# Chunked attention before a SwiGLU-like feed-forward: four 64x64 TensorE tiles, token order by GpSimd, wider v loads, two load queues, and a new order of the first loads

## The chip, the cores and the metric

The kernel runs on one core of a Trainium2 chip. The metric is the device time of one execution in microseconds. The kernel before takes 379.26 us (median of 3 runs, 377.64 to 379.83). A run over 1.5% above the fastest of its kernel counts as slow and is left out. The span that a profile shows is about 2 us shorter than the timed run (377.2 against 378.91 us in the profiled run of before).

## The reference, cut to what matters

```python
batch, n_heads, seq, head_dim = (8, 8, 576, 64)          # attention in chunks of 64 tokens, 9 per sequence
scores = scale * np.matmul(q_c, k_c.transpose(0, 1, 2, 4, 3))     # 64x64 for each chunk and head
attn = np.exp(scores - max) / sum
out = np.matmul(attn, v_c)
# then, over all 8*576 = 4608 tokens, with x = out of all heads side by side (4608 x 512):
h = x @ w_in                                             # 512 -> 2048
g = h * (1.0 / (1.0 + np.exp(-beta * h)))
return (g @ w_out).astype(np.float32)                    # 2048 -> 512
```

All inputs and the output are float32; the kernel multiplies in bfloat16. q, k and v are 9.4 MB each, w_in and w_out 4.2 MB each.

## The kernel before

The tokens are cut into 9 blocks of 512 (8 chunks of 64, all 8 heads). For each block the kernel loads q, k and v, casts them, transposes q and k so that the head dimension lies on the partitions, computes scores, exponentials, V products and their normalization into `xT`, and then two large products: `mm1` (w_in, 16 groups of 4 matmuls) and `mm2` (w_out, the same size). Instructions are emitted in the order of an invented time, `at(time, f, ...)`; every engine runs its own in that order and waits on semaphores for what it needs. One unit of that time is one group of mm1 and, from block 1 on, one group of mm2. So the schedule is a static order for each engine, and an instruction that waits holds up all that follow it on the same engine.

```python
def load_qk(blk, h0, n_h):                  # q on partitions 0-63, k on 64-127; 8 tokens (2 KB) in a piece
    ...
        r = 64 * which + 8 * at
        return e.dma_start(qkstage[r:r + 8 * n, s, h0:h0 + n_h, :],
                           a.rearrange("h (p i) d -> p h (i d)", i=8))
    P.dma("sp", f, ...)
...
def order_k(blk, hp, eng):                  # k alone is put into token order; q is read with a stride
    P.op(eng, lambda e: e.tensor_copy(
        kT[:, hp, :, :, :].rearrange("k c p i -> k (c p) i"),
        qkT[:, :, hp, 64:128].rearrange("k i t -> k t i")), ...)
...
def scores(blk, hp):
    for c in range(8):
        for hb in range(2):                 # two diagonal tiles: rows r and columns r
            r = slice(64 * hb, 64 * hb + 64)
            e.matmul(A[r, hp, 64 * c:64 * c + 64],
                     kT[r, hp, c, :, :].rearrange("k p i -> k (p i)"),
                     qkT[r, :, hp, 8 * c:8 * c + 8].rearrange("k i p -> k p i"))
...
# first loads: q, k, v of block 0; w_in; q, k, v of block 1; then w_out
at(-96, load_qk, 1, 0, 8)
at(-95, load_v, 1)
```

The softmax here doesn't subtract the row's maximum and nothing guards it: scores larger than these inputs give would overflow.

Of the kernel before, what the change touches and what calls it, by code (L numbers as in the profile page):

```python
# [157 lines left out]
def bass_chunk_attention__then__act_swish_beta_kernel(nc, q, k, v, w_in, w_out, beta, out):  # L158
# [8 lines left out]
    with ExitStack() as es:  # L167
# [7 lines left out]
        selsum = sb("selsum", [128, 8], F32)  # L175
        sel = sb("sel", [128, 8, 64], BF16)
# [9 lines left out]
        vstage = sb("vstage", [128, NVS, 4, 8, 64], F32)  # L186
        qkcast = sb("qkcast", [128, 8, H, 64], BF16)
        qkT = sb("qkT", [128, 8, 4, 128], BF16)
        kT = sb("kT", [128, 4, 8, 8, 8], BF16)
        NVA = 2  # L190
        v_bf = sb("v_bf", [128, NVA, 4, 8, 64], BF16)
# [27 lines left out]

        def make_constants():  # L220
# [6 lines left out]
            for b in range(4):  # L227
# [5 lines left out]
            ident = identity[:, :].rearrange("p (m g x y) -> p m g x y", m=4, g=2, x=2)  # L233
            P.op("dve", lambda e: e.tensor_reduce(
                selsum[:, :], ident[:, :, 0, :, :].rearrange("p m x y -> p y m x"),
                mybir.AxisListType.XY, ALU.add), reads=[K("identity")], writes=[K("selsum")])
            P.op("dve", lambda e: e.tensor_single_scalar(
                sel[:, :, :], selsum[:, :].unsqueeze(2).to_broadcast([128, 8, 64]), -1.0, ALU.mult),
                reads=[K("selsum")], writes=[K("sel")])
            P.op("dve", lambda e: e.tensor_reduce(  # L240
                mask[:, :], ident[:, :, :, 1, :].rearrange("p m g y -> p m g y"),
                mybir.AxisListType.XYZ, ALU.add), reads=[K("identity")], writes=[K("mask")])
# [12 lines left out]
        def load_qk(blk, h0, n_h):  # L255
            s = blk % NQS
            for which, src in ((0, q), (1, k)):
                for b, c, n, at in chunk_runs(blk):
                    def f(e, which=which, src=src, b=b, c=c, n=n, at=at):
                        a = src[b][h0:h0 + n_h, 64 * c:64 * (c + n), :]  # L260
                        r = 64 * which + 8 * at
                        return e.dma_start(qkstage[r:r + 8 * n, s, h0:h0 + n_h, :],  # L262
                                           a.rearrange("h (p i) d -> p h (i d)", i=8))
                    P.dma("sp", f, writes=[K("qkstage", s, hp, which, at, v=blk)
                                           for hp in range(h0 // 2, (h0 + n_h) // 2)])

        def load_v(blk):
            s = blk % NVS
            for b, c, n, at in chunk_runs(blk):
                for h in range(H):  # L270
                    def f(e, b=b, c=c, n=n, at=at, h=h):
                        a = v[b, h][64 * c:64 * (c + n), :]
                        r = 64 * (h % 2)
                        return e.dma_start(vstage[r:r + 64, s, h // 2, at:at + n, :],  # L274
                                           a.rearrange("(c j) d -> j c d", j=64))
                    P.dma("sp", f, writes=[K("vstage", s, at, h, v=blk)])
# [29 lines left out]
        def cast_w_out(j, engines):  # L306
            s = (4 + j) % NWS
            for i, eng in enumerate(engines):
                dst = w_out_bf[:, 4 * j + i, :]
                src = wstage[:, s, 512 * i:512 * (i + 1)]  # L310
                if eng == "act":
                    P.op("act", lambda e, d=dst, a=src: e.activation(d, a, AF.Copy, scale=0.5),
                         reads=[K("wstage", s, v=4 + j)], writes=[K("w_out", 4 * j + i)])
                else:
                    P.op(eng, lambda e, d=dst, a=src: e.tensor_single_scalar(d, a, 0.5, ALU.mult),  # L315
                         reads=[K("wstage", s, v=4 + j)], writes=[K("w_out", 4 * j + i)])
# [22 lines left out]
        def order_k(blk, hp, eng):  # L339
            P.op(eng, lambda e: e.tensor_copy(  # L340
                kT[:, hp, :, :, :].rearrange("k c p i -> k (c p) i"),
                qkT[:, :, hp, 64:128].rearrange("k i t -> k t i")),
                reads=[K("qkT", hp, v=blk)], writes=[K("kT", hp, v=blk)])

        def transpose_pe(blk, hp, eng):
            dst = A[:, hp, :].bitcast(BF16).rearrange("p (i t) -> p i t", i=8)
            for i in range(8):
# [3 lines left out]
                    reads=[K("qkcast", hp, v=blk), K("identity")], writes=[K("A", hp, v=("t", blk))])  # L351
            for which, out, src in (
                    ("kT", kT[:, hp, :, :, :].rearrange("k c p i -> k (c p) i"),
                     dst[:, :, 64:128].rearrange("k i t -> k t i")),
                    ("qkT", qkT[:, :, hp, 0:64], dst[:, :, 0:64])):
                if eng == "act":
                    P.op("act", lambda e, out=out, src=src: e.activation(out, src, AF.Copy),
                         reads=[K("A", hp, v=("t", blk))], writes=[K(which, hp, v=blk)])
                else:
                    P.op("dve", lambda e, out=out, src=src: e.tensor_copy(out, src),  # L360
                         reads=[K("A", hp, v=("t", blk))], writes=[K(which, hp, v=blk)])

        def cast_v(blk, eng, hp):
            s, sa = blk % NVS, blk % NVA
            keys = [K("vstage", s, at, h, v=blk) for _, _, _, at in chunk_runs(blk)
                    for h in (2 * hp, 2 * hp + 1)]
            P.op(eng, lambda e: e.tensor_copy(v_bf[:, sa, hp, :, :], vstage[:, s, hp, :, :]),  # L367
                 reads=keys, writes=[K("v_bf", sa, hp, v=blk)])

        def scores(blk, hp):  # L370
            for c in range(8):
                for hb in range(2):
                    def f(e, c=c, hb=hb):
                        r = slice(64 * hb, 64 * hb + 64)
                        return e.matmul(A[r, hp, 64 * c:64 * c + 64],  # L375
                                        kT[r, hp, c, :, :].rearrange("k p i -> k (p i)"),
                                        qkT[r, :, hp, 8 * c:8 * c + 8].rearrange("k i p -> k p i"))
                    P.op("pe", f, reads=[K("qkT", hp, v=blk), K("kT", hp, v=blk)],
                         writes=[K("A", hp, v=("s", blk))])

        def exp(blk, hp):
            P.op("act", lambda e: e.activation(E[:, hp, :], A[:, hp, :], AF.Exp, scale=0.125),  # L382
                 reads=[K("A", hp, v=("s", blk))], writes=[K("E", hp, v=blk)])
# [19 lines left out]
        def spread(blk, hps, banks):  # L403
            for b in range(4):
                for hp, bank in zip(hps, banks):
                    P.op("pe", lambda e, b=b, hp=hp, bank=bank: e.matmul(  # L406
                        A[:, bank, 128 * b:128 * b + 128],
                        sel[32 * hp:32 * hp + 32, 2 * b:2 * b + 2, :].rearrange("p h d -> p (h d)"),
                        Rs[32 * hp:32 * hp + 32, :], tile_position=(32 * hp, 0)),
                        reads=[K("Rs", v=blk), K("sel")], writes=[K("A", bank, v=("r", blk, hp))])  # L410

        def attend(blk, hp, bank):
            sa = blk % NVA
            for c in range(8):
                for hb in range(2):
                    def f(e, c=c, hb=hb):
                        r = slice(64 * hb, 64 * hb + 64)
                        return e.matmul(A[r, bank, 64 * c:64 * c + 64],  # L418
                                        v_bf[r, sa, hp, c, :], E[r, hp, 64 * c:64 * c + 64])
                    P.op("pe", f, reads=[K("E", hp, v=blk), K("v_bf", sa, hp, v=blk)],  # L420
                         writes=[K("A", bank, v=("o", blk, hp))])

        def copy_o(blk, hp, bank):
            P.op("act", lambda e: e.activation(o_sb[:, hp % 2, :], A[:, bank, :], AF.Copy),  # L424
                 reads=[K("A", bank, v=("o", blk, hp))], writes=[K("o_sb", hp % 2, v=(blk, hp))])

        def normalize(blk, hp, bank):
            sx = blk % NXT
            P.op("dve", lambda e: e.tensor_tensor(  # L429
                xT[:, sx, hp, :], o_sb[:, hp % 2, :], A[:, bank, :], ALU.mult),  # L430
                reads=[K("o_sb", hp % 2, v=(blk, hp)), K("A", bank, v=("r", blk, hp))],
                writes=[K("xT", sx, hp, v=blk)])


        def mm1(blk, t, bank):
            sx, sg, T = blk % NXT, blk % 2, NT * blk + t
            for c in range(NC):
# [3 lines left out]
                    reads=[K("w_in", t // 4, c), K("xT", sx, c, v=blk)],  # L441
# [8 lines left out]
        def mm2(blk, s, part, bank):  # L450
# [6 lines left out]
            if part == 3:  # L457
                P.op("act", lambda e: e.activation(ostage[:, N % NOS, :], F[:, bank, :], AF.Copy),  # L458
# [11 lines left out]
        def attention(blk, t0, u):  # L470
# [3 lines left out]
            for hp in range(4):  # L474
# [112 lines left out]
```

## Time and profile before

In the tables and profile lines, PE is TensorE (PEld its weight loads), DVE is VectorE, ACT is ScalarE and POOL is GpSimd; L453 is a line of the kernel, and `[19.19 <-POOL w_out_bf L315]` says that the engine stood idle for 19.19 us before and what ended the wait. A "large matmul" is one of mm1 or mm2; "spread" is the matmuls that copy the reciprocals of the softmax sums over the partitions; beta is the input that scales h in the sigmoid.

| Stretch of the span (us) | What runs | PE busy |
|---|---|---|
| 0-26 | loads, block 0's attention | little |
| 26-61 | block 0's mm1, block 1's attention | 26.3 of 35.1 us |
| 61-82 | wait for w_out, behind q, k, v of blocks 1 and 2 | 1.6 of 20.8 us |
| 82-97 | first mm2 groups, paced by w_out casts | 10.3 of 14.9 us |
| from 97 | mm1 of one block interleaved with mm2 of the one before | 33.5 of 34.0 us for a block |

From the page's busy slices of before (each digit is the busy share of a fortieth of the span in tenths; PEclk is the granted clock of TensorE in tenths; the last row is GB/s):

```profile
PE   1669584026898999999999999999999999999996
...
PEclk9999955558999989999999999999999999999999
DMA  8999999977879988849995994897250100001012
```

The load is busy in all of the first slices while PE has a hole in slices 7 to 9. The stretches (columns: stretch, its length, busy time and count of PE, PE's weight loads, DVE, ACT and POOL, granted clock, DMA share, GB/s) show two loading rates and the full stage:

```profile
15.00:20.00 5.00, 5.00 (x103) 4.80 (x100) 1.88 (x4) 2.43 (x5) 1.23 (x2) 1.00 1.28 234
20.00:25.00 5.00, 2.52 (x63) 1.74 (x59) 3.19 (x5) 1.59 (x3) 0.61 (x1) 1.00 1.05 386
...
199.00:233.00 34.00, 33.47 (x287) 17.38 (x290) 14.84 (x23) 17.20 (x28) 11.41 (x14) 1.00 0.81 159
```

The timeline of PE shows what ended the hole, and the chain of waits one block's scores:

```profile
82.10 2.06 PE L453 MATMUL F<-w_out_bf,g 128*128 128x512 bf16 x4 [19.19 <-POOL w_out_bf L315]
```

```profile
199.04 3.63 PE A L375 x64
```

In the trace these 64 matmuls start in pairs 110 ns apart, while pairs of V products, whose operands are dense, start some 30 ns apart.

### The profile page before, as it was taken

How to read it: one execution, taken by the hardware profiler on the slowest of the kernel's cores; microseconds unless marked ns; L12 is line 12 of the kernel's file. 1: busy time of each engine (PE TensorE's matmuls, PEld its weight loads, DVE VectorE, ACT ScalarE, POOL GpSimd, SP SyncE). 2: the span in 40 equal slices, each digit the busy share in tenths (PEclk: the TensorE clock that was granted, in tenths of full speed). 3: DMA queues.
4: the chain of work that ended last, by engine and by line, in shares of the span. 5: the costliest groups of instructions: out<-in, count | busy, mean ns of one | idle time of the engine just before them, and what ended most of it. 6: DMA issues, size and time to landing. Idle time of an engine off the chain costs nothing.

```text
span 377.2 us, 6314 instructions
## 1 busy us (share of the span) xinstructions
PE 320.5 (85%) x2621; PEld 166.1 (44%) x2656; DVE 148.3 (39%) x245; ACT 167.9 (45%) x271; POOL 95.2 (25%) x111
## 2 busy tenths in 40 slices
PE   1669584026898999999999999999999999999996
PEld 0544272001364544464446445544644464444442
DVE  2357625002325426433642454255236425544310
ACT  2438462002454345536553654545365536444521
POOL 0211230069643364063042405226040000000000
PEclk9999955558999989999999999999999999999999
DMA  8999999977879988849995994897250100001012
GB/s 151 201 385 195 153 298 261 143 113 156 160 179 198 207 184 189 178 118 202 138 176 123 188 181 113 176 202 155 61 108 30 56 22 36 30 28 57 28 56 85
DMA packets 89053, 53.91 MB, mean 143 GB/s; under 512 B 71104, under 2 KB 71104, under 8 KB 89024
## 3 DMA queue, kind: packets, MB, share of 16 engines
q1 hardware_dynamic: 81776, 44.05, 59.0%
q10 hardware_dynamic: 7248, 9.45, 8.0%
q8 instruction: 21, 0.34, 0.4%
q14 instruction: 8, 0.07, 0.1%
HBM read 36.71 MB, written 9.44 MB: 122 GB/s over the span
## 4 chain that ended last, share of the span: by engine, by line
PE 72%; SPq 14%; DMA 6%; DVE 3%; issue 2%; POOL 2%; ACT 1%; POOLq 0%
PE F L453 32%; PE F L438 29%; SPq L274 8%; PE A L375 7%; DMA qkstage<-in_k_dram 5%; SPq L262 5%; PE A L418 2%; PE A L406 1%; POOL w_out_bf L315 1%; POOL qkcast L329 1%; ACT tt L443 1%; DVE g L446 1%; DMA vstage<-in_v_dram 1%; SPq L283 1%; PE A L388 1%
## 5 line engine op out<-in xcount | busy, mean ns | idle before, releaser
L446 DVE SCALAR_TENSOR_TENSOR g<-tt,F 128x512 bf16<-128x512 bf16 x144 | 98.7, 687 | 183.8 <-ACT tt L443 183.8
L453 PE MATMUL F<-w_out_bf,g 128*128 128x512 bf16 x553 | 145.0, 384 | 26.6 <-POOL w_out_bf L315 20.9
L443 ACT ACTIVATE tt<-F,beta_half 128x512 bf16<-128x512 f32 x144 | 98.7, 687 | 148.9 <-PE F L438 148.4
L438 PE MATMUL F<-xT,w_in_bf 128*128 128x512 bf16 x564 | 148.6, 389 | 3.1 <-DVE g L446 0.9
L453 PEld LDWEIGHTS F<-w_out_bf,g 128*128 128x128 bf16 x576 | 55.1, 98 | 93.9 <-POOL w_out_bf L315 23.7
L438 PEld LDWEIGHTS F<-xT,w_in_bf 128*128 128x128 bf16 x576 | 55.7, 100 | 70.6 <-issue 5.0
L329 POOL CAST qkcast<-qkstage 128x1024 bf16<-128x1024 f32 x31 | 31.5, 1056 | 105.7 <-DMA qkstage<-in_k_dram 105.7
L340 POOL COPY kT<-qkT 128x512 bf16<-128x512 bf16 x28 | 28.8, 1069 | 49.8 <-DMA qkT<-qkcast 49.8
L375 PE MATMUL A<-qkT,kT 64*64 64x64 bf16 x576 | 33.3, 283 | 0.0
L375 PEld LDWEIGHTS A<-qkT,kT 64*64 64x64 bf16 x576 | 31.0, 127 | 3.4 <-issue 2.1
L458 ACT ACTIVATE ostage<-F 128x512 f32<-128x512 f32 x36 | 21.5, 597 | 22.0 <-PE F L453 22.0
L424 ACT ACTIVATE o_sb<-A 128x512 f32<-128x512 f32 x36 | 21.3, 594 | 13.0 <-PE A L418 7.9
L429 DVE TENSOR_TENSOR xT<-o_sb,A 128x512 bf16<-128x512 f32 x36 | 24.1, 681 | 2.6 <-PE A L406 2.6
L382 ACT ACTIVATE E<-A 128x512 bf16<-128x512 f32 x36 | 21.2, 595 | 7.0 <-PE A L375 3.9
L367 POOL CAST v_bf<-vstage 128x512 bf16<-128x512 f32 x34 | 20.5, 621 | 14.5 <-PE A L375 5.8
L348 PE MATMUL A<-identity,qkcast 128*128 128x128 bf16 x64 | 7.3, 292 | 17.4 <-DVE qkcast L329 8.5
L348 PEld LDWEIGHTS A<-identity,qkcast 128*128 128x128 bf16 x64 | 5.7, 132 | 18.9 <-DVE qkcast L329 8.8
L406 PE MATMUL A<-Rs,sel 32*128 32x128 bf16 x144 | 8.5, 235 | 6.4 <-DVE Rs L399 6.0
L418 PE MATMUL A<-E,v_bf 64*64 64x64 bf16 x576 | 13.9, 204 | 0.0
L418 PEld LDWEIGHTS A<-E,v_bf 64*64 64x64 bf16 x576 | 12.0, 119 | 4.1 <-issue 2.9
L315 POOL TENSOR_SCALAR w_out_bf<-wstage 128x512 bf16<-128x512 f32 x8 | 11.9, 1512 | 0.0
L395 DVE RECIPROCAL R<-A 128x128 f32<-128x128 f32 x9 | 8.6, 952 | 5.5 <-PE A L388 5.5
(30 smaller groups left out, 48.7 us busy)
## 6 DMA issues: line engine op xcount, KB each, us to landing
out_dram<-ostage ACTq DMA_DIRECT2D x36, 256.0 KB, 2.7
wstage<-in_moe_w_in_dram SPq DMA_DIRECT2D x4, 1024.0 KB, 11.0
wstage<-in_moe_w_out_dram SPq DMA_DIRECT2D x4, 1024.0 KB, 9.9
vstage<-in_v_dram SPq DMA_DIRECT2D x16, 128.0 KB, 6.0
qkstage<-in_q_dram SPq DMA_DIRECT2D x2, 896.0 KB
qkstage<-in_k_dram SPq DMA_DIRECT2D x2, 896.0 KB
vstage<-in_v_dram SPq DMA_DIRECT2D x16, 112.0 KB, 4.9
qkstage<-in_q_dram SPq DMA_DIRECT2D x6, 256.0 KB, 10.5
```

The costliest lines, as they stand in the source:

```text
L274: return e.dma_start(vstage[r:r + 64, s, h // 2, at:at + n, :], a.rearrange("(c j) d -> j c d", j=64))
L329: P.op(eng, lambda e: e.tensor_copy(dst, src), reads=keys, writes=[K("qkcast", hp, v=blk)])
L340: P.op(eng, lambda e: e.tensor_copy(kT[:, hp, :, :, :].rearrange("k c p i -> k (c p) i"), qkT[:, :, hp, 64:128].rearrange("k i t -> k t i" ...
L375: return e.matmul(A[r, hp, 64 * c:64 * c + 64], kT[r, hp, c, :, :].rearrange("k p i -> k (p i)"), qkT[r, :, hp, 8 * c:8 * c + 8].rearrange ...
L418: return e.matmul(A[r, bank, 64 * c:64 * c + 64], v_bf[r, sa, hp, c, :], E[r, hp, 64 * c:64 * c + 64])
L424: P.op("act", lambda e: e.activation(o_sb[:, hp % 2, :], A[:, bank, :], AF.Copy), reads=[K("A", bank, v=("o", blk, hp))], writes=[K("o_sb" ...
L429: P.op("dve", lambda e: e.tensor_tensor(xT[:, sx, hp, :], o_sb[:, hp % 2, :], A[:, bank, :], ALU.mult), reads=[K("o_sb", hp % 2, v=(blk, h ...
L438: P.op("pe", lambda e, c=c: e.matmul(F[:, bank, :], w_in_bf[:, c, 128 * t:128 * t + 128], xT[:, sx, c, :], start=(c == 0), stop=(c == NC - ...
L443: P.op("act", lambda e: e.activation(tt[:, T % 3, :], F[:, bank, :], AF.Tanh, scale=beta_half[:, t:t + 1]), reads=[K("F", bank, v=("h", T) ...
L446: P.op("dve", lambda e: e.scalar_tensor_tensor(g2[:, sg, t, :], tt[:, T % 3, :], 1.0, F[:, bank, :], ALU.add, ALU.mult), reads=[K("F", ban ...
L453: P.op("pe", lambda e, t=t: e.matmul(F[:, bank, :], g2[:, sg, t, 128 * s:128 * s + 128], w_out_bf[:, t, :], start=(t == 0), stop=(t == NT ...
L458: P.op("act", lambda e: e.activation(ostage[:, N % NOS, :], F[:, bank, :], AF.Copy), reads=[K("F", bank, v=("o", N))], writes=[K("o", N % ...
```

## The change

The intent: fewer PE microseconds for attention (four 64x64 tiles at once on dense operands, for scores and V products), with GpSimd putting both q and k into token order; earlier loads at the start (q and k of block 0 on two queues, v on 128 partitions with a quarter to a half of the DMAs); and w_out ahead of block 1, so that block 0's mm2 can follow its mm1 while block 1 loads. The core of the diff, cut:

```diff
-        def load_qk(blk, h0, n_h):
+        def load_qk(blk, which, h0, n_h, queue):
...
-                    P.dma("sp", f, ...)
+                P.dma(queue, f, ...)
...
         def load_v(blk):
-                        r = 64 * (h % 2)
-                        return e.dma_start(vstage[r:r + 64, s, h // 2, at:at + n, :],
-                                           a.rearrange("(c j) d -> j c d", j=64))
+                        r = 64 * (at % 2)
+                        return e.dma_start(vstage[r:r + 64 * m, s, at // 2, :, :],
+                                           v[b][:, 64 * c:64 * (c + m), :].rearrange("h t d -> t h d"))
...
-        def order_k(blk, hp, eng):        # 128x512
+        def order_qk(blk, hp, eng):       # 128x1024, q and k
...
         def scores(blk, hp):
+            u, w = divmod(hp, 2)
+            for cc in range(4):
+                for g in range(2):
+                    for hb in range(2):
+                            r, col = slice(64 * hb, 64 * hb + 64), 256 * w + 64 * cc
+                            return e.matmul(A[64 * g:64 * g + 64, 2 * u + hb, col:col + 64],
+                                            qkO[r, hp, 1, 2 * cc + g, :], qkO[r, hp, 0, 2 * cc + g, :])
...
         def attend(...)                    # likewise: rows by chunk g, columns by head hb
         def spread(...)
-                        sel[32 * hp:32 * hp + 32, ...], Rs[32 * hp:32 * hp + 32, :]
+                              sel[:, u, 2 * (2 * w + ch) + g, :], Rs[:, :]       # all 128 rows
...
+            at(-99, load_qk, 0, 0, 2 * hp, 2, "sp")
+            at(-99, load_qk, 0, 1, 2 * hp, 2, "act")
...
-        at(-96, load_qk, 1, 0, 8)
-        at(-95, load_v, 1)
+        at(12, load_qk, 1, 0, 0, 8, "sp")       # behind w_out on the same queue
+        at(15.9, load_qk, 1, 1, 0, 8, "act")
+        at(12.1, load_v, 1)
...
+            return (0, 32)[blk] if blk < 2 else 16 * (blk + 1)      # block 1's mm1 only after block 0's mm2
...
+                at(40.5 if blk == 3 else t0 - 16.9, cast_qk, blk, hp, "pool")
+                at(t0 - 6.5 + 1.25 * hp, order_qk, blk, hp, "pool")
+                at(t0 - 1.2, cast_v, blk, "pool", hp)
```

The factor 0.5 also moves from the w_out casts to the copy of the output, so that GpSimd casts w_out plainly. And block 2's q and k, which a DMA transposed before, are transposed by PE now (96 PE transposes instead of 64).

## The prediction

> **What bounds the kernel now.** From about 97 us on, TensorE: the stretch table has PE busy 33.47 of 34.0 us at 199-233 us. A block there is 128 large matmuls of 0.216 us (27.6 us) plus 6.4 us of attention. The chain of waits shows a block's 64 score matmuls at 3.63 us; in the trace, pairs (two diagonal 64x64 tiles) start every 110 ns, V-product pairs about every 32 ns: score operands are strided, V operands dense. Before 97 us, the load: DMA share is near 1.0 from 5 to 80 us, and the timeline has PE idle from 63 to 82 us, waiting for w_out behind q, k, v of blocks 1 and 2 and GpSimd's w_out casts (1512 ns each, plain casts 615).
>
> **Removed, added, moved.**
> 1. Scores: dense operands, four tiles. If four overlap, 16 groups of about 40 ns, 0.65 us; if only pairs, 1.0 us. Saves 2.5-2.9 us per block; V products 0-0.4. The Trainium skill, "TensorEngine Tiling (Array Packing)", Tile-to-Partition Mapping, lists four independent 64x64 tiles; no run here shows four yet. Spread becomes 16 full-array matmuls instead of row-tiled pairs: +0.45 us. Attention per block 6.4 to about 3.7-4.0 us, all on the path in blocks 3-8: 15 us; blocks 0-2 gain also.
> 2. GpSimd orders 128x1024 instead of 128x512: about 2.1 us instead of 1.07, some 15 us of GpSimd per 31 us block. Off the path.
> 3. Two queues. Loads to 64 partitions move 204-234 GB/s (10-20 us), w_in to 128 partitions 386 (20-25 us). "SBUF — State Buffer", Door 1: The DMA port swizzle, says 64 partitions reach half the ports; this trace agrees. Both halves at once should fill both: last q/k about 9.5 us instead of 13.9, though beta's small packets precede k. v on 128 partitions: 13.5 instead of 19.4. First large matmul about 22 us instead of 26.
> 4. w_out before block 1: w_in in by about 25 us, w_out by 36, cast by 39; mm1 of block 0 ends about 36.5, so its mm2 follows almost unstalled, and block 1's q/k/v (36-47 us) hide under it. Block 1's attention, with PE transposes and little to overlap, stalls 3-5 us. mm1 of block 1 starts about 58-60 us, the interleaved stage about 80-82. Of the 57 us in which PE does little before 97 us, some 40 go.
>
> **Sum.** 81 + 7 x 27.6 (blocks 2-8, each with the mm2 before it) + 6 x 3.9 + 13.8 (last mm2) + 3 drain + 3 small stalls = 318 us span, plus 2 us that the timed run has over the span: 320 us. Range 309 to 336. Faster 0.97, same 0.02, slower 0.01.
>
> **What would show it.** 1: a block's score matmuls under 1.2 us, 64x64 starts in fours, a steady block of 31-32 us. 2: no PE wait on ordered q/k after 100 us. 3: DMA over 300 GB/s before 10 us; first large matmul at 21-24 us. 4: no PE gap above 3 us from 25 to 60 us, no w_out wait above 1 us.
>
> **What would make it wrong.** Four tiles may not overlap (mode switches, shared rows): scores near 2 us, +6 us in all. ScalarE issues block 1's k only after its 16th tanh; if k shares badly with 256-byte v packets, block 1's scores come 5-10 us late, straight on the path. mm1 of block 1 with attention of block 2 loads ScalarE 18 of 20 us. ScalarE's and VectorE's first w_in casts hold back w_out if block 0's attention is late.

## More of the kernel before

One helper matters later. It records which instruction must signal for which:

```python
def _depend(self, op, reads, writes):
    ...
    for key, v in writes:
        add(self.writer.get(key), op["queue"] == "pool")
        for r in self.readers.get(key, ()):     # EVERY reader of a tile signals for its next writer
            add(r, False)
```

## The result, and the profile after

The changed kernel takes 362.65 us (median of 3 runs, 362.6 to 363.2), 0.9575 of before (95% interval 0.9527 to 0.9624). Ratios in this document are the mean time of one kernel's fast runs over the mean of the other's fast runs of the same rounds, so they are not quite the ratio of the medians. It is faster, as predicted, but by 16.6 us instead of 59, and 362.65 lies outside the predicted range of 309 to 336. The same rows of the page, after:

```profile
PE   0559974598768089999899999999999999999996
...
PEclk9999996869969569999999999999999999999999
DMA  8998999998779978899999979981011000001012
```

The hole before block 1 has become several smaller ones (slices 7, 8 and 12 to 14), again with clocks of 0.5 to 0.6, and one slice in which PE does nothing at all (the fourteenth, 117 to 127 us). The stretches, cut where the prediction had its milestones, and one steady block:

```profile
0.00:26.90 26.90, 9.81 (x192) 7.43 (x194) 10.18 (x27) 9.13 (x13) 7.61 (x17) 1.00 1.03 254
26.90:43.30 16.40, 15.41 (x63) 6.46 (x65) 11.16 (x17) 10.95 (x16) 11.71 (x21) 1.00 0.95 307
43.30:79.10 35.80, 24.33 (x252) 13.28 (x257) 8.78 (x12) 9.17 (x15) 6.59 (x9) 0.81 1.08 175
79.10:109.30 30.20, 23.07 (x258) 11.27 (x261) 17.30 (x27) 17.04 (x27) 10.21 (x12) 0.89 0.82 164
...
222.30:254.90 32.60, 31.29 (x284) 15.36 (x288) 14.85 (x23) 17.28 (x28) 13.80 (x12) 1.00 0.74 154
```

Set against the terms of the prediction's sum (318 us of span):

| Stretch | Predicted (us) | Measured (us) | Off by |
|---|---|---|---|
| to the first large matmul | 22 | 26.9 | 4.9 |
| block 0's mm1 | 14.5 (22 to 36.5) | 16.4 | 1.9 |
| block 0's mm2 with block 1's attention | 22.5 (to 59) | 35.8 | 13.3 |
| block 1's mm1 with block 2's attention | 22 (to 81) | 30.2 | 8.2 |
| all the rest | 237 | 252.1 | 15.1 |
| sum | 318 | 361.4 | 43.4 |

The 15.1 us hold an 11.0 us gap in block 3 and 1.1 us in each of four steady blocks (32.6 against 27.6 + 3.9). The first row is a single profile: in e1, e1b, e4 and e6 below, which load and work on block 0 in the same way, the first large matmul comes at 24.97 to 26.08 us, so up to 1.9 of the 4.9 us are scatter between runs. PE's timeline shows where the largest gaps are:

```profile
47.12 0.39 PE L468 MATMUL F<-w_out_bf,g 128*128 128x512 bf16 x1 [1.10 <-POOL w_out_bf L322]
...
58.91 2.74 PE L362 MATMUL A<-identity,qkcast 128*128 128x128 bf16 x24 [5.34 <-DVE qkcast L336]
...
103.46 0.93 PE L416 MATMUL A<-Rs,sel 128*128 128x128 bf16 x7 [2.36 <-DVE xT L441]
...
127.75 0.43 PE L383 MATMUL A<-qkO 64*64 64x64 bf16 x16 [11.02 <-POOL qkO L350]
```

The wait for w_out has gone from 19.19 to 1.10 us, as intended. In its place PE waits 5.34 us for block 1's q and k at 58.9 us (its mm2 groups before that had kept it busy until 53.6), and 11.02 us at 127.75 us for the last of block 3's four orderings by GpSimd. GpSimd's timeline tells what it did meanwhile:

```profile
110.63 5.73 POOL L350 COPY qkO<-qkT 128x1024 bf16<-128x1024 bf16 x3 [6.90 <-PE F L452]
121.86 3.99 POOL L336 CAST qkcast<-qkstage 128x1024 bf16<-128x1024 f32 x4 [5.50 <-DMA qkstage<-in_k_dram]
125.80 1.90 POOL L350 COPY qkO<-qkT 128x1024 bf16<-128x1024 bf16 x1
```

Three orderings, then the casts of block 4, for which GpSimd stood 5.50 us until block 4's k had landed, and only then the fourth ordering.

A steady block shrank from 34.0 to 32.6 us. Its score matmuls now take 1.5 us instead of 3.7, the V products 0.9 instead of 1.4, the spread 1.2 instead of 0.8 (groups of PE in that stretch). Their starts in the trace, for block 6 and for block 8, in ns from the first:

```
block 6:   0 3 6 10 | 52 55 59 62 | 84 87 90 94 | 115 119 122 125 | ... 242 245 249 252 | 274 300 335 369 403 437 471 ... 1325
block 8:   0 4 7 10 | 53 56 60 63 | 85 88 91 95 | 116 120 123 126 | ... 243 246 250 253 | 275 278 281 285 | 306 310 ... 550
```

Four tiles do start together, every 32 ns, for 32 matmuls; then, in blocks 4 to 7, they start singly, every 34 ns. In block 8 they go on in fours until near the end. What differs in block 8 is that there is no next writer of the ordered q and k: 4 of its 64 score matmuls increment a semaphore, 64 of 64 in the blocks before. (In the kernel before, block 8 has only 4 increments too, and its pairs start every 110 ns as in the other blocks: there the increments were not the limit. That the strided operand was, is argued from the dense V pairs of the same trace; no run changes the stride alone.)

### The profile page after: what moved, and what is told of

The parts are those of the page before. It is cut to its first block, busy times and chain, and to the rows that moved or that the text cites. A ratio compares the mean times of both kernels' runs of the same rounds, so it can differ in the third digit from the quotient of the medians.

```text
span 361.4 us, 6228 instructions
## 1 busy us (share of the span) xinstructions
PE 301.7 (83%) x2646; PEld 148.1 (41%) x2688; DVE 148.2 (41%) x234; ACT 165.5 (46%) x262; POOL 115.2 (32%) x126
## 4 chain that ended last, share of the span: by engine, by line
PE 70%; DMA 9%; DVE 6%; ACT 6%; issue 3%; POOL 3%; SPq 2%; ACTq 0%; DVEq 0%; POOLq 0%
PE F L452 31%; PE F L468 28%; DMA qkstage<-in_k_dram 9%; PE A L416 3%; ACT tt L458 3%; PE A L383 3%; ACT E L389 2%; POOL qkcast L336 2%; DVE R L402 2%; PE A L429 2%; PE A L362 1%; SPq L340 1%; DVE g L461 1%; PE A L395 1%; DVE Rs L406 1%
## 5 line engine op out<-in xcount | busy, mean ns | idle before, releaser
L452 PE MATMUL F<-xT,w_in_bf 128*128 128x512 bf16 x552 | 146.0, 390 | 3.5 <-issue 1.6
L350 POOL COPY qkO<-qkT 128x1024 bf16<-128x1024 bf16 x24 | 45.7, 1945 | 59.0 <-PE A L383 29.7
L436 ACT ACTIVATE o_sb<-A 128x512 f32<-128x512 f32 x36 | 20.9, 594 | 16.6 <-PE F L468 5.5
L383 PE MATMUL A<-qkO 64*64 64x64 bf16 x576 | 11.4, 201 | 13.8 <-POOL qkO L350 11.6
L416 PE MATMUL A<-Rs,sel 128*128 128x128 bf16 x144 | 13.4, 243 | 10.7 <-DVE Rs L406 7.1
L416 PEld LDWEIGHTS A<-Rs,sel 128*128 128x128 bf16 x144 | 10.3, 110 | 17.6 <-DVE Rs L406 11.2
L383 PEld LDWEIGHTS A<-qkO 64*64 64x64 bf16 x576 | 9.8, 114 | 17.7 <-POOL qkO L350 11.8
L362 PE MATMUL F<-identity,qkcast 128*128 128x128 bf16 x32 | 4.1, 310 | 12.9 <-DVE qkcast L336 10.9
L322 POOL CAST w_out_bf<-wstage 128x512 bf16<-128x512 f32 x16 | 9.1, 613 | 7.3 <-DMA wstage<-in_moe_w_out_dram 7.3
L336 DVE CAST qkcast<-qkstage 128x1024 bf16<-128x1024 f32 x4 | 3.8, 970 | 16.8 <-DMA qkstage<-in_k_dram 16.8
L362 PE MATMUL A<-identity,qkcast 128*128 128x128 bf16 x64 | 6.2, 266 | 5.3 <-DVE qkcast L336 5.3
## 6 DMA issues: line engine op xcount, KB each, us to landing
vstage<-in_v_dram SPq DMA_DIRECT2D x32, 256.0 KB, 11.9
```

What stands on the lines that cost most here:

```text
L336: P.op(eng, lambda e: e.tensor_copy(dst, src), reads=keys, writes=[K("qkcast", hp, v=blk)])
L350: P.op(eng, lambda e: e.tensor_copy(dst, src), reads, writes)
L383: return e.matmul(A[64 * g:64 * g + 64, 2 * u + hb, col:col + 64], qkO[r, hp, 1, 2 * cc + g, :], qkO[r, hp, 0, 2 * cc + g, :])
L416: return e.matmul(A[:, banks[g], col:col + 128], sel[:, u, 2 * (2 * w + ch) + g, :], Rs[:, :])
L436: P.op("act", lambda e: e.activation(o_sb[:, g, :], A[:, bank, :], AF.Copy), reads=[K("A", bank, v=("o", blk, u))], writes=[K("o_sb", g, v ...
L452: P.op("pe", lambda e, c=c: e.matmul(F[:, bank, :], w_in_bf[:, c, 128 * t:128 * t + 128], xT[:, sx, c, :], start=(c == 0), stop=(c == NC - ...
```

## The experiments

Eleven kernels were run, in three rounds. All gave correct results. Each is an edit of the changed kernel unless it says otherwise, and is timed against the kernel before in the same rounds. The changed kernel itself was timed only with the result (3 runs), and the three submissions ran on three chips. So a gain over the changed kernel, given below as a difference of medians, is uncertain by 1 to 2 us: through the ratios it would be 5.8 us for e1, 9.4 for e1b, 4.4 for e5, 0.3 for e3, 3.0 for e10, 6.5 for e6 and 14.1 for e7. What is said of single waits comes from one profile of each kernel.

| Run | Edit | Median (us) | Ratio to before | 95% interval |
|---|---|---|---|---|
| the change | | 362.65 | 0.9575 | 0.9527-0.9624 |
| e1_pool_order | block 4's q/k casts behind block 3's last ordering | 357.52 | 0.9421 | 0.9364-0.9478 |
| e1b_pool_order_v | and behind block 3's v casts | 354.1 | 0.9328 | 0.9257-0.9399 |
| e5_last_signal | one increment per tile | 359.67 | 0.9458 | 0.9415-0.9502 |
| e3_one_queue | block 0's k on q's queue | 363.64 | 0.9567 | 0.9513-0.9621 |
| e10_beta_late | beta behind block 0's k | 361.8 | 0.9496 | 0.9436-0.9555 |
| e4_block1_first | block 1 ahead of w_out, as before | 366.86 | 0.9628 | 0.9567-0.9688 |
| e6_k_early | block 1's k issued 7 us earlier | 357.32 | 0.9403 | 0.9330-0.9476 |
| e7_qk128 | q and k each over 128 partitions | 349.92 | 0.9202 | 0.9125-0.9279 |
| e8_all | e1b + e5 + e6 + e7 | 339.27 | 0.8935 | 0.8848-0.9021 |
| e9_fill | e8 + block 2's attention spread out | 330.16 | 0.8679 | 0.8608-0.8751 |
| e11_all_beta | e9 + e10 | 328.21 | 0.8613 | 0.8544-0.8682 |

### GpSimd's order (e1_pool_order, e1b_pool_order_v)

```diff
-                at(40.5 if blk == 3 else t0 - 16.9, cast_qk, blk, hp, "pool")
+                at(40.5 if blk == 3 else max(t0 - 16.9, 49.3), cast_qk, blk, hp, "pool")
```

Block 3's attention starts at another offset than the others', so that its fourth ordering (invented time 49.25) stood behind block 4's casts (48.6).

> Only change: GpSimd casts q/k of block 4 after it has ordered the fourth head pair of block 3, not before. Theory A (program order): the 11.0 us gap of PE at 116.9-127.8 us comes from GpSimd standing in that cast, which waits for the q/k load of block 4, with block 3's last ordering queued behind it. Then the gap falls below 2 us and the time is 350 to 354 us. Rival B (the data or GpSimd's work of block 3 is itself late): a gap of more than 5 us stays and the time is over 357 us.

Measured: 357.52 us, and GpSimd's timeline is as theory A has it for the orderings, but with a new victim of the same cast:

```profile
109.38 7.60 POOL L350 COPY qkO<-qkT 128x1024 bf16<-128x1024 bf16 x4 [6.91 <-PE F L452]
120.91 4.00 POOL L336 CAST qkcast<-qkstage 128x1024 bf16<-128x1024 f32 x4 [3.93 <-DMA qkstage<-in_k_dram]
124.85 2.30 POOL L350 CAST v_bf<-vstage 128x512 bf16<-128x512 f32 x4
```

All four orderings now run in one piece, and the largest gap of PE there fell from 11.0 to 1.5 us. But block 3's v casts stood behind block 4's q/k casts as well, and PE's first V product waited for them until 125.6 us. So only 5.1 of the 11 us came out: the gap fell as theory A had it, and the time (over 357 us) is the one that theory B had named, for another reason. The second edit moves the casts to 50.9 and block 4's transpose to 51.5:

> As e1_pool_order, and the casts of block 3's v on GpSimd are also put ahead of the q/k casts of block 4 (whose DMA transpose moves with them). In e1 the first V product of block 3 waited for those v casts until 125.6 us, and GpSimd had stood until 120.9 us for block 4's q/k load. Theory A: the same head-of-line wait; PE's idle in block 3 falls by a further 3 to 5 us and, with less time at half clock, the time is 350 to 354 us. Rival B (v of block 3 itself lands late, after 120 us): the time stays at 356 to 359 us.

Measured: 354.1 us, just over theory A's range; the wait for v is gone. From block 3's first score to block 4's is 32.0 us (41.2 in the changed kernel, 37.4 in e1). That profiled run has a 3.2 us wait for reciprocals in block 5's attention (at 196 us) that the steady blocks of the others don't have; it was not looked into. The gap is settled as GpSimd's program order: 8.5 us by the medians.

### Increments (e5_last_signal)

```diff
-            for r in self.readers.get(key, ()):
-                add(r, False)
+            readers = self.readers.get(key, ())
+            last_pe = [r for r in readers if r["queue"] == "pe"][-1:]
+            for r in [r for r in readers if r["queue"] != "pe"] + last_pe:
+                add(r, False)
```

> Only change: of the matmuls that read a tile, only the last one increments PE's semaphore for the tile's next writer, instead of each. In the changed kernel the scores of blocks 4 to 7 start in fours every 32 ns for the first 32 matmuls, then singly every 34 ns (1.33 us for 64), but those of block 8, whose matmuls carry 4 increments instead of 64, stay in fours (0.55 us). Theory A (increments serialise): all blocks show about 0.55-0.65 us, a steady block goes from 32.6 to about 31.8 us, the time is 355 to 359 us. Rival B (the queue of instructions ahead of PE is drained after 64 of them, or loads and GpSimd, which are quiet in block 8, slow PE's reads): blocks 4 to 7 stay at 1.3 us and the time at 361 to 364 us.

Measured: scores of blocks 4 to 7 start in fours for the first 52 of 64 (the last 12 follow singly, about 8 ns apart) and take 0.58 us from first to last start instead of 1.33. Their groups in a steady block, in the changed kernel and in e5:

```profile
L383 PE MATMUL A<-qkO 64*64 64x64 bf16 x64 | 1.5, 191 | 0.0
```

```profile
L385 PE MATMUL A<-qkO 64*64 64x64 bf16 x64 | 0.8, 195 | 0.0
```

Two of the four steady periods are 31.84 us, the others 32.1 and 32.4. So theory A holds and theory B falls: loads and GpSimd are as busy as before, and only increments were taken away (those of all other matmuls that share a tile, too). The time is 359.67 us, 3 us less and just short of the expected 355 to 359. The 0.75 us comes only in blocks 4 to 7 (4 x 0.75 = 3.0 us; the four periods are 2.7 us shorter together), not in block 8, which had it already, nor fully in the first blocks, where PE waits for other things.

The Trainium skill has the mechanism: "TensorE: Matmul & The Clock Gate", The cost: per-tile semaphore tail, says that increments serialize, with 26.3 ns for each in its fit, and that one on the last tile is enough. This trace agrees in kind, with 34 ns for each matmul once the first 32 are out.

### Does the second queue bring anything? (e3_one_queue, e10_beta_late)

```diff
-            at(-99, load_qk, 0, 1, 2 * hp, 2, "act")
+            at(-99, load_qk, 0, 1, 2 * hp, 2, "sp")
```

> Only change: k of block 0 goes on the same queue as q, as before the change. Theory A (two queues bring no bandwidth): the trace of the changed kernel has q and k packets of 2 KB at 142 to 147 ns each and 240 GB/s together, against 223-225 GB/s on one queue before; so the last q/k cast starts within 1 us of the changed kernel's 14.9 us and the time is 361 to 365 us. Rival B (two queues do help and something else hid it): q/k come over 3 us later and the time is over 365 us.

Measured: 363.64 us, and the last q/k cast at 14.71 us (14.92 with two queues, 13.86 before). Theory A holds: two queues as the change has them bring nothing that shows beyond the scatter (in e1, e1b, e4 and e6, with two queues, that cast starts at 13.79 to 13.95 us). One reason was visible in the trace: beta, a load of 2048 packets of 4 bytes, stands ahead of k on ScalarE's queue, and no packet of k is recorded before about 5 us. So e10 lets beta follow k (and moves the halving of beta down VectorE's order):

```diff
-        at(-100, load_beta)
+        at(-98.5, load_beta)
+        at(-32, halve_beta)
```

> The changed kernel; only change: beta, 2048 packets of 4 bytes, is loaded behind k of block 0 on ScalarE's queue and not ahead of it. In the changed kernel no k packet of block 0 is recorded before about 5 us, when beta's are through. Theory A (k's late start is why the two queues gained nothing at the start): last q/k cast of block 0 at 13 us or earlier instead of 14.9, first large matmul at or before 25.4 instead of 26.9, time 359 to 362 us. Rival B (q and k to half the partitions each are limited to about 240 GB/s together anyhow): the last cast stays after 14 us, the time at 362 to 364 us.

Measured: 361.8 us, first k packet at 3.31 us instead of 5.08, last q/k cast at 12.45 us, first large matmul at 25.06 us. The cast comes 1.3 us before the earliest and 2.5 us before the latest of the kernels with beta ahead of k, so that part of theory A is shown. That the first large matmul gains by it is not: 25.06 us lies within the 24.97 to 26.90 us of those kernels. One reason is in the trace: beta's packets now run beside v, which comes at 151 GB/s from 11 to 14 us (214 from 13 to 16 us in the changed kernel), and PE waits 1.4 us for v's casts. The 0.9 us by the medians are within the uncertainty.

Do two queues bring bandwidth, once beta is out of the way? From 6 to 9 us almost only q and k are under way. In the order: e3 (one queue), the changed kernel (two), and from 8 to 10 us e10 (two):

```profile
6.00:9.00 3.00, 0.55 (x6) 0.56 (x7) 0.87 (x2) 0.00 (x0) 0.00 (x0) 1.00 1.07 226
```

```profile
6.00:9.00 3.00, 0.00 (x0) 0.00 (x0) 0.26 (x2) 0.00 (x0) 0.00 (x0) 1.00 1.07 241
```

```profile
8.00:10.00 2.00, 0.00 (x0) 0.00 (x0) 0.00 (x0) 1.33 (x2) 0.00 (x0) 1.00 1.04 303
```

In the changed kernel two queues bring 6 to 7% (241 against 226, and 228 GB/s in before). But this is not a fixed limit: e6, with the same start, has 272 GB/s from 6 to 9 us, and e10 reaches 303. Why the same pair of loads runs faster in one run than in another (247 in e5 and 262 in e1, on one chip) was not found. The stretch of 4 to 8 us, in the order: the change, e10, and e11 (which has q and k over 128 partitions, too):

```profile
4.00:8.00 4.00, 0.00 (x0) 0.00 (x0) 0.17 (x1) 1.28 (x1) 0.00 (x0) 1.00 1.06 197
```

```profile
4.00:8.00 4.00, 1.04 (x8) 0.77 (x8) 0.69 (x1) 1.99 (x2) 0.00 (x0) 1.00 1.01 239
```

```profile
4.00:8.00 4.00, 1.62 (x13) 1.18 (x14) 0.76 (x2) 2.82 (x4) 0.00 (x0) 1.00 1.08 357
```

197, 239 and 357 GB/s: with two halves on two queues and beta out of the way there are 239 in this stretch, with both tensors over all partitions 357.

### q and k over 128 partitions (e7_qk128)

```diff
-        qkstage = sb("qkstage", [128, NQS, H, 512], F32)
+        qkstage = sb("qkstage", [128, NQS, 2, H, 256], F32)
...
-                    r = 64 * which + 8 * at
-                    return e.dma_start(qkstage[r:r + 8 * n, s, h0:h0 + n_h, :],
-                                       a.rearrange("h (p i) d -> p h (i d)", i=8))
+                    r = 16 * at
+                    return e.dma_start(qkstage[r:r + 16 * n, s, which, h0:h0 + n_h, :],
+                                       a.rearrange("h (p i) d -> p h (i d)", i=4))
...      # casts split by q and k; transposes and orderings re-indexed, same number and size
```

> Only change: q and k each lie over all 128 partitions (4 tokens, 1 KB, in a piece) instead of 64 partitions each (8 tokens, 2 KB); same bytes, same number of DMAs, transposes and matmuls, twice the casts of half the size. Theory A (half the partitions are half the write bandwidth, and that is what made q/k late, not the queues): q and k come at 300 GB/s or more, the last q/k cast of block 0 starts before 11 us instead of 14.9, the first large matmul at 22-24 us instead of 26.9, q/k of block 1 land by 48 us instead of 58; time 335 to 350 us. Rival B (the source side or the number of packets limits): q/k stay under 250 GB/s, the time is over 356 us.

Measured: 349.92 us, at the upper end of theory A's range and far from B's. At the start theory A's numbers were wrong: the last q/k cast began at 14.65 us, the first large matmul at 26.3 us. q ran first (291 GB/s in all from 4 to 6 us, on one queue); k, behind beta, recorded its first packet at 6.52 us and shared the time to 11.9 us with v (291 GB/s together from 6.5 to 12 us). With beta behind k (e11) the last cast starts at 10.06 us and the first large matmul at 22.3 us (24.7 in e9, the same kernel with beta ahead), which is what the prediction had said for the change itself, without this layout. In the middle, block 1's k was cast at 55.0 us instead of 58.2 (A had said 48), and block 4's q and k landed early enough that GpSimd's wrong order cost almost nothing: 30.9 us from block 3's first score to block 4's, with no order changed. The gains of e1b and e7 are thus in part the same microseconds.

### Block 1's loads (e4_block1_first, e6_k_early)

```diff
-        at(12, load_qk, 1, 0, 0, 8, "sp")
-        at(15.9, load_qk, 1, 1, 0, 8, "act")
-        at(12.1, load_v, 1)
+        at(-96, load_qk, 1, 0, 0, 8, "sp")
+        at(-96, load_qk, 1, 1, 0, 8, "sp")
+        at(-95, load_v, 1)
```

> Only change: q, k and v of block 1 are loaded ahead of w_out, as before the change; all else stays. Theory A (what counts is the 14.7 MB that block 1's first matmul needs, whatever their order; the order only moves the wait): PE's wait for q/k at 53-59 us goes, a wait for w_out of 8 to 15 us comes in its place, block 1's first large matmul stays within 4 us of 79 us, and the time is 358 to 367 us. Rival B (w_out first is what gained): the time is 370 us or more.

Measured: 366.86 us. The time lies in theory A's range, but its reason was wrong. The wait came where A said, but block 1's first large matmul came at 90.9 us and not within 4 us of 79:

```profile
52.97 2.19 PE L468 MATMUL F<-w_out_bf,g 128*128 128x512 bf16 x4 [10.02 <-POOL w_out_bf L322]
...
64.06 8.20 PE L468 MATMUL F<-w_out_bf,g 128*128 128x512 bf16 x24 [3.22 <-POOL w_out_bf L322]
```

So loading w_out first is worth 12 us at that point (12 to 15 against the six kernels that load w_out first and issue k late: it comes at 76.2 to 79.1 us in the changed kernel, e1, e1b, e3, e5 and e10), which B had claimed. The later start then hides GpSimd's wrong order in block 3: from block 3's first score to block 4's is 31.8 us in e4 and 41.2 in the changed kernel. Of the 12 us that the new load order gains, 9.4 are given back there; this is one place where the expected gain went.

```diff
-        at(15.9, load_qk, 1, 1, 0, 8, "act")
+        at(8, load_qk, 1, 1, 0, 8, "act")
```

> Only change: ScalarE issues the k load of block 1 before the ninth tanh of block 0, about 7 us earlier, not after the sixteenth, so that q and k of block 1 are in flight together behind w_out. Theory A (k is late because it is issued late, and q and k then come one after the other): last q/k of block 1 lands at 50-53 us instead of 58, the time is 355 to 359 us. Rival B (loads of 64 partitions or fewer are limited to 140-240 GB/s whichever queue and order): it lands at 55 us or later, the time is 360 to 364 us.

Measured: theory A holds. The last q/k of block 1 is there at 50.6 us instead of 58.2, the time is 357.32 us. Block 1's first large matmul comes 8.9 us earlier (70.2 us against 79.1; 6 us before the earliest of the same six kernels), but the gap in block 3 is 3.5 us worse (44.7 us from block 3's first score to block 4's), so 5.3 us remain. In the changed kernel q of block 1 came first, then k, issued by ScalarE only with its sixteenth tanh at 42.66 us; with v's packets beside them, slices of 2.5 us from 41 to 58.5 us show 132 to 230 GB/s. In e6 both were in flight together and one slice of 2.5 us (44 to 46.5) shows 346 GB/s. Why two partial loads together got so much more there than at the start was not tested.

### All together, and what was left (e8_all, e9_fill, e11_all_beta)

> The four corrections together: q and k over 128 partitions, block 1's k issued early, GpSimd's order of blocks 3 and 4, one semaphore increment per tile. If their causes are independent, the gains add: about 5 us (increments), 8 (GpSimd's order), 15 to 25 (loads): 325 to 340 us. If they hide each other behind one common wait (the total bytes before block 1), 340 to 350 us.

Measured: 339.27 us, 23.4 us less than the changed kernel. The single gains by the medians are 8.5 (e1b), 3.0 (e5), 5.3 (e6) and 12.7 (e7), 29.5 us together; they overlap by some 6 us (10 if the gains are taken through the ratios). The time is at the upper end of what independence had been expected to give.

In e8 block 1's mm1 with block 2's attention still took 32.2 us (70.0 to 102.1 us). PE's groups in that stretch, in e8:

```profile
L415 PE MATMUL A<-Rs,sel 128*128 128x128 bf16 x16 | 2.2, 306 | 4.9 <-DVE xT L440 2.9 <-DVE Rs L405 2.0
L428 PE MATMUL A<-E,v_bf 64*64 64x64 bf16 x64 | 1.3, 218 | 0.7 <-ACT E L388 0.7
L382 PE MATMUL A<-qkO 64*64 64x64 bf16 x64 | 0.9, 195 | 1.1 <-DVE qkO L348 1.1
```

(After the second bar: PE's idle time before them, and on what.) PE, ScalarE and VectorE wait for each other in turn, because this attention is squeezed into 7.3 steps of mm1 alone, where the steady blocks have 12 steps of mm1 and mm2.

```diff
-            at(34 + hp, cast_qk, 2, hp, "pool")
-            at(35.5 + hp, transpose_pe, 2, hp, A, "A", ("act", "dve")[hp % 2])
-            at(38.7, cast_v, 2, "pool", hp)
-        attention(2, 39.5, 0.6)
+            at(32.3 + 0.4 * hp, cast_qk, 2, hp, "pool")
+            at(33.5 + 0.7 * hp, transpose_pe, 2, hp, A, "A", ("act", "dve")[hp % 2])
+            at(37, cast_v, 2, "pool", hp)
+        attention(2, 36.2, 0.85)
...      # in attention(): everything from the sums on 0.5 later
```

> As e8_all, with the attention of block 2 started 3.3 steps earlier and spread over 10.7 steps instead of 7.3 in the sixteen first products of block 1, and in every block all of the attention after the exponentials half a step later. In e8, block 1's first products with block 2's attention take 30 us (70 to 100 us) where PE has 21 us of work at full clock; PE waits there for normalized x, reciprocals and exponentials in turn. Theory A (too little other work between the steps of a serial chain): the stretch falls to 22-26 us, a steady block from 31.8 to about 31.2 us, time 328 to 335 us. Rival B (ScalarE or VectorE is full in that stretch): it stays at 28 us or more, time 336 to 341 us.

Measured: 330.16 us, within theory A's range. The stretch itself, up to block 1's first mm2, takes 27.7 us instead of 32.2, between what A (22 to 26) and B (28 or more) had said; to block 3's first score it is 33.9 us instead of 38.3. So it gained some 4.4 us, less than expected; steady blocks went from 31.8 to 30.8 us, more than expected. Also, the granted clock of that profiled run is 1.00 over the whole span (0.953 in the changed kernel, 0.979 in e8). That is no more than one profile: e11, whose gaps after 20 us are no longer (2.4 us at most, 2.7 in e9), has two stretches of 3.4 us at half clock and 0.989. The two parts of the edit (block 2's start, the half step in all blocks) were not run apart.

> e9_fill and e10_beta_late together. With 128-partition loads q ran at 258 GB/s alone in e7 while k waited behind beta, then k alone. Theory A of e10: 1.5 to 3 us less than e9_fill. Theory B: within 1 us of e9_fill.

Measured: 328.21 us, 2 us less than e9, as theory A says (single runs overlap: 327.59 to 329.7 against 329.28 to 333.79), and 0.8613 of before. Its stretches, and a late steady block in which PE is busy throughout:

```profile
0.00:22.30 22.30, 10.06 (x192) 7.19 (x193) 9.09 (x26) 8.90 (x14) 6.15 (x16) 1.00 1.06 279
22.30:41.20 18.90, 17.24 (x67) 6.85 (x66) 12.23 (x19) 11.38 (x17) 13.13 (x24) 1.00 1.00 318
41.20:66.20 25.00, 21.14 (x256) 10.97 (x257) 9.23 (x14) 9.27 (x16) 7.23 (x12) 0.93 1.14 246
66.20:95.30 29.10, 22.31 (x262) 11.13 (x261) 17.47 (x26) 16.76 (x27) 14.14 (x21) 0.94 1.04 189
...
222.70:253.50 30.80, 30.80 (x290) 14.74 (x289) 14.79 (x24) 17.05 (x28) 9.91 (x8) 1.00 0.10 36
```

## Why the prediction was right or wrong

The prediction had the direction and the bounds of the kernel before right. It was 42.65 us too low, and its sum failed in five terms:

1. **Step 1, scores and V products: right in mechanism, wrong in size.** Four tiles do overlap (starts in fours every 32 ns; 40 were assumed), and V products and spread came as costed. But a block's scores take 1.5 us instead of 0.65, because each of their 64 matmuls increments a semaphore and they start singly after 32 of them (shown by e5: 0.8 us without). A steady block took 32.6 us, not 31 to 32; besides the increments, 0.4 us each of waiting for exponentials and reciprocals was there and was not in the sum. e9, in which these steps come half a step later, has 30.8 us.
2. **Step 2, "Off the path": wrong.** GpSimd's load was as predicted (1945 ns for an ordering, about 2.1 us said; 13.8 us in a steady block) and it is idle more than half of the time. What counted was its order: one ordering behind a cast that waits for a load, 11.0 us of PE. The prediction added up GpSimd's work and never laid its program order against the arrival of the loads. "No PE wait on ordered q/k after 100 us" was its own test, and it failed. e1 and e1b take 8.5 us of it back.
3. **Step 3, "Both halves at once should fill both": wrong.** One queue does as well (e3). Two things stood in the way. k stood behind beta, which the prediction had named and thought small: its first packet came at 5.08 us, 3.31 without (e10), and the last q/k cast 1.3 to 2.5 us later; what this costs at the first large matmul doesn't show with 64 partitions and is 2.4 us with 128 (24.7 in e9, 22.3 in e11). And two half loads at once reached 241 GB/s in the changed kernel and not the 386 of w_in. The skill's page that was cited for it, "SBUF — State Buffer", says in another section ("Can I just issue two DMAs to hit both halves?") that two such loads measured only 6% over one; it was there to be read. Here they bring 6 to 7% in the changed kernel (241 against 226 GB/s from 6 to 9 us), though up to 303 GB/s in e10: what limits them stays open. Both tensors over 128 partitions, with beta behind k, reach 357 GB/s and the first large matmul at 22.3 us (e11), where the prediction had put it; that is another layout than it had reckoned with.
4. **Step 4, w_out first: half right.** The wait for w_out did go (19.19 to 1.10 us), and e4 shows that the new order is worth 12 us at block 1's first large matmul. "Block 1's q/k/v (36-47 us) hide under it" was wrong: they were cast at 58.2 us, since q and k came one after the other at 132 to 230 GB/s with v beside them, k issued at 42.66 us. The danger was named ("ScalarE issues block 1's k only after its 16th tanh ... 5-10 us late, straight on the path") but not put into the sum; e6 takes 8.9 us of it back at that point. With block 1's attention squeezed into the second half of mm2, the stretch took 35.8 us and not 22.5; in e11 it is 25.0.
5. **Block 1's mm1 with block 2's attention: 30.2 us instead of 22.** The prediction counted PE's work and ScalarE's ("18 of 20 us") but not the serial chain through PE, ScalarE and VectorE. ScalarE was busy for 17.0 of 30.2 us, so it was not the limit; giving the chain more steps of other work took 4.4 us back (e9). The stretch was still 29.1 us in e11, so most of this term is not recovered, and what bounds it there is open.

Gaps also cost more than their length. In the changed kernel PE's clock was granted at half in four stretches of 6.8, 6.8, 6.8 and 13.7 us, 34 us in all; there a group of four large matmuls takes up to 1.91 us instead of 1.03. Two of them begin during the gaps of 5.3 and 11.0 us, the other two where the longest gaps near them are 1.8 and 2.4 us. The Trainium skill, "TensorE: Matmul & The Clock Gate", Part 1, has such a rule (a window of about 3.4 us without work halves the clock), and the trace agrees in the length of the steps, all multiples of 3.4 us; the gaps of 1.8 and 2.4 us are shorter than its window. The prediction left this out of the sum.

All edits together (e11) give 328.21 us, near the predicted 320. But e11 also has q and k over 128 partitions and block 2's attention spread out, which the prediction had not, so no run shows that its own steps, each working, would reach 320. The sum added what the parts could do and left out who waits in line for whom.

## What to carry to other kernels

On an engine that runs in order, being mostly idle says nothing: for each instruction that waits for a load, look at what stands behind it in that engine's order, and put it behind the work that is already possible. When several small matmuls share a tile, let only the last reader signal. Lay a load over all 128 partitions before thinking of a second queue, and look at what else stands ahead on that queue: 8 KB of 4-byte packets can delay a megabyte.

## What the Trainium skill lacked or had wrong

- "TensorE: Matmul & The Clock Gate", The cost: per-tile semaphore tail: it gives the tail of one group of tiles. It doesn't say what a long stream does: here 32 matmuls with an increment each started in fours every 32 ns, and those after them singly every 34 ns, until most increments were taken away (1.33 to 0.58 us for 64).
- "TensorEngine Tiling (Array Packing)": no rate is given for four 64x64 tiles. Here four dense 64-column matmuls start every 32 ns, and pairs of two diagonal tiles about as often; with a strided moving operand a pair started every 110 ns, for which no page gives a rate (that the stride is the cause was not isolated).
- "SBUF — State Buffer", "Can I just issue two DMAs to hit both halves?": its 6% is what the changed kernel shows (241 against 226 GB/s), but as a general answer it is too low: two half loads reach 303 GB/s in e10 (8 to 10 us) and 346 GB/s in one 2.5 us slice of e6. This was not explained.
- "DMA: Bandwidth & Descriptors": that a load of tiny packets ahead on the same queue delays the next load is not there with a number. Here 2048 packets of 4 bytes (beta) were through at about 5 us, and k, behind them, recorded its first packet then.
- No page works through the case in which an idle engine's program order holds up the critical one; here it was 11.0 us of PE, and GpSimd was busy 32% of the span.
